# Linformer attention and squared-ReLU FFN on one core: TensorE order of the first two batches' attention rearranged, V copies of the first batch on VectorE, rest of Q loaded ahead of the last w_out piece

## The chip, the core and the metric

The kernel runs on one core of one Trainium2 chip. The metric is device time in microseconds (us).

## The reference

Eight batches, eight heads, 1024 tokens of 64 elements. Keys and values are projected from 1024 positions to 64, then comes attention, then a two-layer FFN over all tokens:

```python
k_proj = einsum('ks,bhsd->bhkd', E, k);  v_proj = einsum('ks,bhsd->bhkd', F, v)
attn = softmax(q @ k_proj.T / 8)                 # 1024 x 64 for each head
x = (attn @ v_proj) -> (8192, 512)
out = square(maximum(x @ w_in, 0)) @ w_out       # 512 -> 2048 -> 512, float32
```

## The kernel before

TensorE's instruction order is written by hand; the other engines are ordered by a scheduler. The FFN of a batch is 64 numbered steps: for each half `c` of the tokens, 16 steps of the first layer (four matmuls each) and 16 of the second layer (four each). The attention of the next batch is hung between those steps with `at(step, stage)`, which puts a stage behind the matmuls of its step. The code is condensed here. In batch 0 steps 1 to 16 are the first layer of half 0, steps 17 to 32 its second layer, 33 to 48 and 49 to 64 the same for half 1.

```python
aps = ctx.enter_context(tc.tile_pool(name="aps", bufs=2, space=PSUM))   # attention: 2 tiles of 2 banks
fps = ctx.enter_context(tc.tile_pool(name="fps", bufs=4, space=PSUM))   # FFN and the rest: 4 single banks
# ... loads, all but that of E on the GpSimd queue, in this order:
#     K0,Q0 first heads | K0,Q0 other heads | F | V0 x2 | w_in x5 | w_out x4 | rest of Q0 | K1 V1 Q1 | K2 V2 Q2 ...

def keep_k(self, ps_k, h=slice(0, 8), second=None):          # k projection out of PSUM, twice
    nc.vector.tensor_copy(self.kp[:, h, 0, :], view)
    (second or nc.vector.tensor_copy)(self.kp[:, h, 1, :], view)   # batch 0: second = nc.scalar.copy
def keep_v(self, ps_v, h=slice(0, 8)):
    nc.scalar.copy(self.vp[HI, h], view)
    nc.vector.tensor_copy(self.vp[LO, h], view)

def inverse(self, ps):                           # 1 / sum of the exponentials, on ScalarE
    nc.scalar.activation(rs[:], ps[:], AF.Ln)
    nc.scalar.activation(rs[:], rs[:], AF.Exp, scale=-1.0)

def values(self, pr, spare=False):
    e = self.e.pop(pr)
    ps_s = att_psum();  self.sums_mm(ps_s, e);  rs = self.inverse(ps_s)
    ps_x = [bank(), bank()] if spare else att_psum()
    # ... 4 matmuls into ps_x, then VectorE: xT = ps_x * rs

def store(self, c, tb, ps):                      # after each 128 rows of the output
    nc.scalar.copy(o[:], ps[:])
    nc.sync.dma_start(out_rows[self.b, i, :, :], o[:])
# ... the front, and batch 0's plan: shown in the diff below
```

Q1, V1 and so on stand for the tensors of batch 1; Q0 for those of batch 0. "The rest of Q" is the half of Q0 that belongs to the tokens of half 1.

The softmax here doesn't subtract the row's maximum and nothing guards it: scores larger than these inputs give would overflow.

## Time and profile before

The median is 522.35 us over three runs (522.2 to 522.53); the profiled span is 521.1 us.

| reading | view | value |
|---|---|---|
| TensorE busy | page, part 1 | 506.3 us of 521.1 |
| named waits of TensorE | waits | 11.1 us |
| of these, rest of Q | waits | 2.9 us, once |
| of these, attention PSUM held by the Ln | waits | 2.0 us, twice |
| after the last matmul | timeline | 3.6 us |
| rest of Q lands, last w_out piece lands | issue plus time to landing | 42.5, 40.0 us |
| Q1 lands | the same | 59.2 us |

These are the busy line of TensorE and the chain that ended last, from the page of the kernel before:

```profile
PE 506.3 (97%) x2764; PEld 223.8 (43%) x2764; DVE 174.7 (34%) x367; ACT 287.1 (55%) x428; POOL 32.2 (6%) x44
PE 90%; DMA 7%; POOL 1%; ACT 1%; DVE 0%; issue 0%; POOLq 0%
```

These are TensorE's waits in the same run (who waited, for whom, total us, times, longest us):

```profile
PE ps_bank L216 <- DMA Q_sb<-in_q_dram: 2.9, 1, 2.9
PE ps_att L241 <- ACT rs L260: 2.0, 2, 1.0
...
PE ps_bank L327 <- DVE xT L310: 1.1, 2, 0.9
...
PE ps_bank L206 <- ACT kp L171: 0.4, 1, 0.4
```

TensorE is the bound, so each of these waits is on the chain as long as nothing later waits anyway. The two upper ones look like this in the timeline (start us, duration us, engine, line, operation, in brackets the idle time before it and who ended it). First the rest of Q, at steps 19 and 20:

```profile
38.68 1.03 PE L333 MATMUL ps_bank<-w_out_126,hsq 128*128 128x512 bf16 x4
42.57 0.62 PE L216 MATMUL ps_bank<-ident,Q_sb 128*128 128x128 bf16 x8 [2.86 <-DMA Q_sb<-in_q_dram]
43.02 1.03 PE L333 MATMUL ps_bank<-w_out_126,hsq 128*128 128x512 bf16 x4
43.89 0.61 PE L216 MATMUL ps_bank<-ident,Q_sb 128*128 128x128 bf16 x8
44.33 1.89 PE L333 MATMUL ps_bank<-w_out_128,hsq 128*128 128x512 bf16 x8
```

Four matmuls of w_out end at 39.7; then TensorE is idle until Q lands, transposes it in two groups with four matmuls between, and is at step 21 at 44.33. Second, one of the two waits for the Ln (the other is like it, 0.91 us at 81.1):

```profile
74.88 0.41 PE L247 MATMUL ps_att<-expT,ones 64*64 64x512 bf16 x4
75.12 0.39 PE L281 MATMUL ps_att<-expT,vp 64*64 64x512 bf16 x4
76.55 0.41 PE L241 MATMUL ps_att<-qT,kT 64*64 64x512 bf16 x4 [1.04 <-ACT rs L260]
```

The scores (L241) need an attention PSUM tile, but the sums just written are still being read by the Ln on ScalarE, one microsecond long.

### The profile page before, as it was taken

The page shows a single profiled execution, that of the slowest core. Times are in us where ns is not written, and L with a number is a line of the kernel's source. Part 1 is how long each engine was busy: PE and PEld are TensorE (multiplying, and loading weights), DVE is VectorE, ACT ScalarE, POOL GpSimd, SP SyncE. Part 2 cuts the span into 40 slices and gives each one's busy share as a digit, 9 for nine tenths or more (in the row PEclk, how much of TensorE's full clock was granted, in tenths as well). Part 3 has the DMA queues.
Part 4 walks back from the last instruction along what each step waited for, and adds up shares of the span by engine and source line. Part 5 has one row for each costly group of instructions (what it writes and reads, how often), then busy time and mean ns, then how long its engine had stood idle before and what let it go on. Part 6 is the DMA issues. An engine that isn't in the chain of part 4 may idle for free.

```text
span 521.1 us, 6860 instructions
## 1 busy us (share of the span) xinstructions
PE 506.3 (97%) x2764; PEld 223.8 (43%) x2764; DVE 174.7 (34%) x367; ACT 287.1 (55%) x428; POOL 32.2 (6%) x44
## 2 busy tenths in 40 slices
PE   7897999999999999999999999999999999999997
PEld 3443443444444444444444444444444444444443
DVE  2351552433513244142431325232440424313130
ACT  1563475574735667276654756356662766544351
POOL 6420100120200020000100000000000000000000
PEclk9899999999999999999999999999999999999999
DMA  9999999999995099104851050110101011010102
GB/s 154 205 205 206 241 207 186 135 207 206 185 191 127 25 179 202 69 13 79 170 97 60 1 142 21 40 42 20 62 1 60 21 40 42 20 62 20 62 0 81
DMA packets 64975, 53.26 MB, mean 102 GB/s; under 512 B 26416, under 2 KB 56624, under 8 KB 64944
## 3 DMA queue, kind: packets, MB, share of 16 engines
q0 software_dynamic: 30880, 29.49, 36.1%
q1 hardware_dynamic: 34064, 23.34, 16.0%
q8 instruction: 21, 0.34, 0.3%
q14 instruction: 10, 0.08, 0.1%
HBM read 59.24 MB, written 16.78 MB: 146 GB/s over the span
## 4 chain that ended last, share of the span: by engine, by line
PE 90%; DMA 7%; POOL 1%; ACT 1%; DVE 0%; issue 0%; POOLq 0%
PE ps_bank L333 43%; PE ps_bank L327 40%; DMA Q_sb<-in_q_dram 4%; DMA w_in_116<-in_moe_w_in_dram 3%; PE ps_bank L182 2%; PE ps_att L247 2%; PE ps_att L241 2%; PE ps_att L281 1%; PE ps_bank L281 0%; PE ps_bank L206 0%; ACT rs L260 0%; POOL Q_sb L76 0%; POOL K_sb L76 0%; POOL V_sb L76 0%; PE ps_bank L216 0%
## 5 line engine op out<-in xcount | busy, mean ns | idle before, releaser
L323 ACT ACTIVATE h_relu<-ps_bank 128x512 bf16<-128x512 f32 x256 | 151.3, 599 | 63.7 <-PE ps_bank L327 62.8
L324 DVE TENSOR_TENSOR hsq<-h_relu 128x512 bf16<-128x512 bf16 x256 | 108.8, 425 | 195.0 <-ACT h_relu L323 193.7
L333 PEld LDWEIGHTS <-hsq 128*128 128x128 bf16 x1024 | 97.6, 98 | 123.2 <-issue 9.3
L340 ACT COPY o_sb<-ps_bank 128x512 f32<-128x512 f32 x64 | 37.3, 586 | 114.8 <-PE ps_bank L333 114.8
L333 PE MATMUL ps_bank<-w_out_128,hsq 128*128 128x512 bf16 x256 | 65.7, 380 | 0.0
L333 PE MATMUL ps_bank<-w_out_124,hsq 128*128 128x512 bf16 x256 | 65.6, 379 | 0.0
L333 PE MATMUL ps_bank<-w_out_126,hsq 128*128 128x512 bf16 x256 | 65.6, 379 | 0.0
L333 PE MATMUL ps_bank<-w_out_130,hsq 128*128 128x512 bf16 x256 | 65.4, 379 | 0.0
L327 PE MATMUL ps_bank<-xT,w_in_122 128*128 128x512 bf16 x256 | 59.2, 379 | 0.0
L327 PE MATMUL ps_bank<-xT,w_in_118 128*128 128x512 bf16 x256 | 58.2, 379 | 0.1
L327 PE MATMUL ps_bank<-xT,w_in_120 128*128 128x512 bf16 x256 | 58.0, 379 | 0.0
L260 ACT ACTIVATE rs<-ps_att 128x1024 f32<-128x1024 f32 x32 | 32.7, 1024 | 23.2 <-PE ps_att L247 23.1
L327 PEld LDWEIGHTS <-w_in_120 128*128 128x128 bf16 x256 | 25.0, 98 | 30.4 <-issue 0.4
L327 PEld LDWEIGHTS <-w_in_118 128*128 128x128 bf16 x256 | 24.9, 98 | 30.1 <-issue 0.4
L327 PEld LDWEIGHTS <-w_in_122 128*128 128x128 bf16 x256 | 24.4, 98 | 30.8 <-issue 2.7
L255 ACT ACTIVATE expT<-ps_att 128x1024 bf16<-128x1024 f32 x32 | 31.8, 1023 | 10.1 <-PE ps_att L241 10.1
L285 DVE TENSOR_TENSOR xT<-ps_att,rs 128x512 bf16<-128x512 f32 x32 | 20.6, 686 | 44.6 <-ACT rs L261 44.6
L261 ACT ACTIVATE rs<-rs 128x1024 f32<-128x1024 f32 x32 | 33.8, 1059 | 0.6
L285 DVE TENSOR_TENSOR xT<-ps_bank,rs 128x512 bf16<-128x512 f32 x24 | 15.5, 686 | 50.5 <-ACT rs L261 50.5
L327 PE MATMUL ps_bank<-xT,w_in_114 128*128 128x512 bf16 x128 | 30.6, 379 | 1.1 <-DVE xT L310 1.1
L327 PE MATMUL ps_bank<-xT,w_in_116 128*128 128x512 bf16 x128 | 30.4, 379 | 0.0
L327 PEld LDWEIGHTS <-w_in_114 128*128 128x128 bf16 x128 | 12.4, 98 | 16.1 <-issue 1.7
(64 smaller groups left out, 203.5 us busy)
## 6 DMA issues: line engine op xcount, KB each, us to landing
out_dram<-o_sb SPq DMA_DIRECT2D x64, 256.0 KB, 2.0
K_sb<-in_k_dram POOLq DMA_DIRECT2D x7, 1024.0 KB, 17.9
V_sb<-in_v_dram POOLq DMA_DIRECT2D x7, 1024.0 KB, 23.7
Q_sb<-in_q_dram POOLq DMA_DIRECT2D x7, 1024.0 KB, 10.8
K_sb<-in_k_dram POOLq DMA_DIRECT2D x2, 512.0 KB, 8.0
V_sb<-in_v_dram POOLq DMA_DIRECT2D x2, 512.0 KB, 12.0
Q_sb<-in_q_dram POOLq DMA_DIRECT2D x2, 256.0 KB, 8.3
w_in_118<-in_moe_w_in_dram POOLq DMA_DIRECT2D x1, 512.0 KB, 15.1
```

The source lines that it names most:

```text
L182: nc.tensor.matmul(ps[LO, :], lhsT=ET[:, i, :], rhs=self.K[:, :, i, :], start=f, stop=l)
L241: nc.tensor.matmul(ps[o, par], lhsT=self.kT[r, h, :], rhs=self.qT[r, h, n, :], start=True, stop=True)
L247: nc.tensor.matmul(ps[o, par], lhsT=ones[r, :], rhs=e[r, par], start=True, stop=True)
L255: nc.scalar.activation(e[:], ps[:], AF.Exp, scale=SCALE)
L260: nc.scalar.activation(rs[:], ps[:], AF.Ln)
L261: nc.scalar.activation(rs[:], rs[:], AF.Exp, scale=-1.0)
L285: nc.vector.tensor_tensor(out=self.xT[:, pr, :, par], in0=ps_x[par].rearrange("p (c t) -> p c t", c=2), in1=rs[:, par].rearrange("p (c t) ...
L323: nc.scalar.activation(r[:], ps[:], AF.Relu)
L324: nc.vector.tensor_tensor(out=self.hsq[c][:, fb, :], in0=r[:], in1=r[:], op=ALU.mult)
L327: nc.tensor.matmul(ps[:], lhsT=w_in_blk(cb, fb), rhs=self.xT[:, cb, c].rearrange("p a t -> p (a t)"), start=(cb == 0), stop=(cb == NCB - 1),)
L333: nc.tensor.matmul(ps[:], lhsT=self.hsq[c][:, fb, tb * P:(tb + 1) * P], rhs=w_out_blk(fb), start=(fb == 0), stop=(fb == NFB - 1),)
L340: nc.scalar.copy(o[:], ps[:])
```

## The change

The intent is to take these two waits away, and to close small gaps in the front with warm-up matmuls and a better order. The diff, with cuts marked:

```diff
     for j in range(WP):
+        if j == WP - 1:
+            load(Q0[:, :, 4:8, :], tokens(q, 0, i=slice(4, 8)))
         t = wpool.tile([P, fn, DM], BF16, name=f"w_out_{j}")
         load(t[:], w_out_view[:, j * fn:(j + 1) * fn, :])
-    load(Q0[:, :, 4:8, :], tokens(q, 0, i=slice(4, 8)))
# ...
-        def keep_v(self, ps_v, h=slice(0, 8)):
+        def keep_v(self, ps_v, h=slice(0, 8), first=None):
-            nc.scalar.copy(self.vp[HI, h], view)
+            (first or nc.scalar.copy)(self.vp[HI, h], view)
# ... in project_v, batch 0 only:
-            self.keep_v(ps[HI, 0:C // 2], half[g])
+            self.keep_v(ps[HI, 0:C // 2], half[g], nc.vector.tensor_copy)
# ... the front:
-        warm(4)
+        warm(8)
         ET = projection("ET", e_bf)
-        warm(8)
+        warm(3)
         att.project_k(0)
         att.transpose_q_chunk(0, Q0, 0)
         att.transpose_k(half[0])
+        warm(1)
         att.chunk_scores(0, 0)
+        warm(2)
         att.project_k(1)
+        att.chunk_sums(0, 0)
         att.transpose_q_chunk(0, Q0, 1)
-        att.chunk_sums(0, 0)
         att.transpose_k(half[1])
+        warm(1)
         att.chunk_scores(0, 1)
         FT = projection("FT", f_bf)
+        warm(3)
+        att.chunk_sums(0, 1)
         att.project_v(0)
-        att.chunk_sums(0, 1)
+        warm(2)
         att.chunk_values(0, 0)
+        warm(2)
         att.project_v(1)
# ... batch 0's plan:
-                at(19, att.transpose_q_chunk, 1, Q0, 0)
+                at(20, att.transpose_q_chunk, 1, Q0, 0)
                 at(20, att.transpose_q_chunk, 1, Q0, 1)
                     at(36, nxt.project)
-                    at(36, nxt.transpose_q, 0), at(36, nxt.transpose_q, 1)
+                    at(37, nxt.transpose_q, 0), at(37, nxt.transpose_q, 1)
                     at(39, nxt.transpose_k)
-                    scores 0, 1 at 42; transpose_q 2 at 44, 3 at 45
-                    values 0 and scores 2 at 47; values 1 and scores 3 at 50; values 2 at 55, 3 at 60; no spare banks
+                    scores 0, 1 at 41; transpose_q 2 and 3 at 43
+                    values 0 at 45; scores 2 at 49; values 1 (spare) and scores 3 at 51
+                    values 2 (spare) at 55, values 3 (spare) at 59
-                        at(60, coming.project), at(62, coming.transpose_q_dma)
+                        at(61, coming.project), at(63, coming.transpose_q_dma)
                         at(64, coming.transpose_k)
```

The last part is told in short form. From batch 1 on the plan is the same as before.

More of the change, by code (lines that the diff above doesn't have):

```diff
@@ L433 @@
                     at(36, nxt.project)
-                    at(36, nxt.transpose_q, 0)
-                    at(36, nxt.transpose_q, 1)
+                    at(37, nxt.transpose_q, 0)
+                    at(37, nxt.transpose_q, 1)
                     at(39, nxt.transpose_k)
-                    s1, s2, s3, s4, s5 = 42, 47, 50, 55, 60
-                    at(44, nxt.transpose_q, 2)
-                    at(45, nxt.transpose_q, 3)
-                else:
-                    s1, s2, s3, s4, s5 = 14, 18, 24, 30, 49
-                at(s1, nxt.scores, 0)
-                at(s1, nxt.scores, 1)
-                spare = b > 0
-                at(s2, nxt.values, 0, spare)
-                at(s2, nxt.scores, 2)
-                at(s3, nxt.values, 1, spare)
-                at(s3, nxt.scores, 3)
-                at(s4, nxt.values, 2)
-                at(s5, nxt.values, 3)
+                    at(41, nxt.scores, 0)
+                    at(41, nxt.scores, 1)
+                    at(43, nxt.transpose_q, 2)
+                    at(43, nxt.transpose_q, 3)
+                    at(45, nxt.values, 0)
+                    at(49, nxt.scores, 2)
+                    at(51, nxt.values, 1, True)
+                    at(51, nxt.scores, 3)
+                    at(55, nxt.values, 2, True)
+                    at(59, nxt.values, 3, True)
+                else:
+                    at(14, nxt.scores, 0)
+                    at(14, nxt.scores, 1)
+                    at(18, nxt.values, 0, True)
+                    at(18, nxt.scores, 2)
+                    at(24, nxt.values, 1, True)
+                    at(24, nxt.scores, 3)
+                    at(30, nxt.values, 2)
+                    at(49, nxt.values, 3)
                 if b + 2 < B:
                     if b == 0:
-                        at(60, coming.project)
-                        at(62, coming.transpose_q_dma)
+                        at(61, coming.project)
+                        at(63, coming.transpose_q_dma)
                         at(64, coming.transpose_k)
                     else:
-                        at(s4, coming.project)
+                        at(30, coming.project)
                         at(27, coming.transpose_q_dma)
-                        at(s5, coming.transpose_k)
+                        at(49, coming.transpose_k)
             for step, _ in enumerate(Ffn(att, b == 0).steps(), 1):
```

## The prediction

> **What bounds the kernel.** TensorE: the busy table gives PE 506.3 us of a 521.1 us span (97%), and the chain of waits is 90% PE. Its 14.8 us of idle time is 11.1 us of named waits (the waits view) plus a tail of 3.6 us (the last matmul ends at 517.5). From batch 1 on there is nothing to win (PE busy 61.0 of 61.0 us in the windows view, 97 to 158), and that schedule stays. So the change can only take waits of the first 85 us: rest of Q 2.9 us (until 42.6); att-PSUM held by the Ln of a softmax 2.0 us (1.04 at 75.5, 0.91 at 80.2); e_bf 1.9; xT 1.1; kT 0.8; FT 0.5; kp 0.4; vp 0.3.
>
> **What the change does.**
>
> 1. Rest of Q one place earlier in the load queue. Loads land in turn: w_out's last piece at 40.0 us (issued 21.05, 18.9 to landing), rest of Q at 42.5 (22.35 + 20.2). Swapped, Q should land near 40.0 and that w_out piece near 42.5. TensorE needs the piece about 43: it just fits. Both Q transposes now follow step 20, so four more matmuls (0.86 us) stand before them. Before, TensorE was through all this at 44.3. After, it comes to the transposes at 36.95 + 16 x 0.216 = 40.4 if the front gains nothing, never before 40.0; done at 40.9 to 41.3. Gain 3.0 to 3.4 us.
>
> 2. The front. Warm-up matmuls are 8+3 rather than 4+8, plus a few in gaps. 128x512 matmuls run 0.43 us apart cold and 0.216 warm here, as in the Trainium skill ("TensorE: Matmul & The Clock Gate", the clock gate: 426.7 and 215.7 ns). The first K projection starts about 1.2 us earlier (8.0, when K lands, instead of 9.17), but the second half of K (12.4), of V (19.5) and w_in (20.8, 22.1) still land as before, so little carries through. V copies were already one after the other (ScalarE 0.37, then VectorE 0.43); both on VectorE take the same, but ScalarE is free for the inverse (ended at 22.9, should end near 20). Projections of V run warm (1.1 instead of 1.4 to 1.6 us). I expect 0 to 0.6 us at step 5; anything above 0.4 is eaten by the wait for Q.
>
> 3. Second half of batch 0. Values stand further from scores and take their PSUM from the spare banks, so the two waits for Ln (1.95 us) go. Waits for banks behind copies may give back 0.2 to 0.6. Batch 1's Q landed at 59.2; its transposes come at about 59.6: little or no wait. All of it is on TensorE, so on the critical path.
>
> The sum: 3.2 + 1.95 - 0.3 = about 4.9 us.
>
> **Predicted time: 517.4 us, range 516.2 to 519.0 (8 in 10). Chances: faster by over 2% 0.01, within 2% 0.98, slower 0.01.**
>
> **What would show it.** In the waits view the wait for Q falls from 2.9 to under 0.5 us and "<- ACT rs" from 2.0 to under 0.3; w_out's last piece lands 2.5 us later than before with no wait for it; the granted clock from 13 to 26 us rises from 0.87 to above 0.95; step 21 starts near 41 instead of 44.3; from batch 1's FFN on, TensorE's timeline is shifted by about 5 us.
>
> **What would make it wrong.** The swapped piece of w_out, or batch 1's Q, arrives late and becomes the new wait; warm matmuls hold up real work; bank waits eat the Ln gain.

## The result, and the profile after

The changed kernel took 518.88 us (median of four runs, 518.74 to 520.21), the kernel before 522.36 us in the same job. The ratio is 0.9939, with a 95% interval of 0.9922 to 0.9956. A ratio here is the mean time of one kernel's fast runs over the mean of the other's fast runs of the same rounds, so it is not quite the ratio of the medians. In a second job (six runs, beside eleven of before) the changed kernel took 519.11 us and the ratio was 0.9924. The gain is 3.5 to 3.8 us by the medians; 4.9 us was predicted. 518.88 is at the slow edge of the predicted range, 519.11 just outside it; that the change is worth less than 2% was predicted too.

Line numbers of the changed kernel are one higher than before (L217 is the old L216, and so on). Its page has these lines:

```profile
PE 507.5 (98%) x2774; PEld 224.2 (43%) x2774; DVE 175.7 (34%) x369; ACT 286.1 (55%) x426; POOL 31.9 (6%) x44
PE 87%; DMA 11%; POOL 1%; issue 0%; ACT 0%; POOLq 0%
```

Its waits of TensorE:

```profile
PE ps_bank L191 <- DMA K_sb<-in_k_dram: 1.7, 1, 1.7
...
PE ps_bank L328 <- DVE xT L311: 1.1, 2, 0.9
PE ps_bank L207 <- ACT kp L172: 0.8, 1, 0.8
PE ps_bank L183 <- ACT o_sb L341: 0.6, 1, 0.6
...
PE ps_bank L227 <- DMA Q_sb<-in_q_dram: 0.6, 1, 0.6
```

Both waits that the change aimed at are gone: there is no line for L217 that waits for the rest of Q, and none for L242 that waits for the Ln. In their place one line has grown and two are new: L207 behind a copy of k on ScalarE (0.8 us; before, it was 0.4 and for the first four heads, while the second four, which wait now, did not wait), L183 behind an output copy (0.6), and L227 behind Q1 (0.6). The first line, a wait for the first K, is an accident of this run (below). Step 21 in the timeline, and the new wait for Q1:

```profile
39.91 1.89 PE L334 MATMUL ps_bank<-w_out_126,hsq 128*128 128x512 bf16 x8
41.64 1.06 PE L217 MATMUL ps_bank<-ident,Q_sb 128*128 128x128 bf16 x16
42.53 1.89 PE L334 MATMUL ps_bank<-w_out_128,hsq 128*128 128x512 bf16 x8
...
61.90 1.07 PE L227 MATMUL ps_bank<-ident,Q_sb 128*128 128x128 bf16 x16 [0.57 <-DMA Q_sb<-in_q_dram]
```

TensorE came to the rest of Q at 41.64 and did not wait; step 21 begins at 42.53, which is 1.8 us sooner than before and not the 3 us predicted. This first profile is of the slowest of the four runs (520.21 us). In it the first K landed at 8.45 us, not at 7.85 as in the profile of before, and the later loads 0.3 to 1.3 us late. So the first thing to settle was what a usual run looks like.

### The profile page after: what moved, and what is told of

The parts are those of the page before. It is cut to its first block, busy times and chain, and to the rows that moved or that the text cites. A ratio compares the mean times of both kernels' runs of the same rounds, so it can differ in the third digit from the quotient of the medians.

```text
span 518.4 us, 6881 instructions
## 1 busy us (share of the span) xinstructions
PE 507.5 (98%) x2774; PEld 224.2 (43%) x2774; DVE 175.7 (34%) x369; ACT 286.1 (55%) x426; POOL 31.9 (6%) x44
## 4 chain that ended last, share of the span: by engine, by line
PE 87%; DMA 11%; POOL 1%; issue 0%; ACT 0%; POOLq 0%
PE ps_bank L334 40%; PE ps_bank L328 39%; DMA Q_sb<-in_q_dram 8%; DMA w_in_122<-in_moe_w_in_dram 3%; PE ps_bank L183 2%; PE ps_att L248 2%; PE ps_att L242 1%; PE ps_bank L282 1%; PE ps_att L282 1%; PE ps_bank L207 0%; PE ps_bank L227 0%; POOL K_sb L76 0%; ACT o_sb L341 0%; ACT rs L261 0%; POOL Q_sb L76 0%
## 5 line engine op out<-in xcount | busy, mean ns | idle before, releaser
L286 DVE TENSOR_TENSOR xT<-ps_bank,rs 128x512 bf16<-128x512 f32 x30 | 19.3, 686 | 60.2 <-ACT rs L262 60.2
L286 DVE TENSOR_TENSOR xT<-ps_att,rs 128x512 bf16<-128x512 f32 x26 | 16.8, 687 | 33.0 <-ACT rs L262 33.0
```

The lines of the kernel that those rows point to most:

```text
L286: nc.vector.tensor_tensor(out=self.xT[:, pr, :, par], in0=ps_x[par].rearrange("p (c t) -> p c t", c=2), in1=rs[:, par].rearrange("p (c t) ...
```

## The experiments

Medians and ranges are of five or six runs unless said otherwise; the kernel before ran eleven times beside each of the first three groups, with medians of 522.94, 523.34 and 522.91 us. Times of different groups may differ by a few tenths for that reason.

My theory after the first profile had three parts. First, the front was not made faster, since the earlier sums put an Ln in front of the second k copy. Second, a PSUM bank held by an output copy costs 0.6 us at step 61. Third, the landing of Q1 now stops TensorE. The main rival was that all of this was one unlucky run.

### r_after: the changed kernel again

No edit.

> The changed kernel again, unedited. Its one profile so far was of a run of 520.2 us, its other three runs took 518.7 to 519.0. In that profile the loads landed 0.6 us late from the first one on and 1.3 us late from w_in on, and TensorE was still cold at the first K projection; step 5 began 1.24 us later than before. Theory A (the front itself was made slower, by about 0.8 us: ScalarE now runs the first Ln ahead of the second kp copy, and the V projection now waits for the softmax sums): this profile shows the kp wait of 0.8 us again, and step 5 begins at 27.2 to 27.9. Theory B (that profile was only an unlucky run): loads land as before (Q's rest at 40.0), step 5 begins at 26.0 to 26.6, and a gain of 1.2 us more than in the first profile. Time 518.8 either way.

Measured: 519.11 us (518.58 to 519.76), ratio 0.9924. The profile is of the run of 518.58 us, span 516.8. Its waits of TensorE, cut:

```profile
PE ps_bank L328 <- DVE xT L311: 1.1, 2, 0.9
PE ps_bank L207 <- ACT kp L172: 0.8, 1, 0.8
PE ps_bank L183 <- ACT o_sb L341: 0.6, 1, 0.6
```

The k wait and the bank wait are there again, and the waits for DMA are not. Loads were early (first K at 7.34, rest of Q at 39.57), and step 21 began at 41.51. Step 5 began at 26.80, in the range of neither theory. So the first profile's late loads were chance, and the two waits behind ScalarE are not. The k wait is explained by ScalarE's order. This is ScalarE before:

```profile
14.34 0.36 ACT L171 CAST kp<-ps_bank 64x256 bf16<-64x256 f32 x1 [0.40 <-DVE kp L170]
14.79 1.02 ACT L260 ACTIVATE rs<-ps_att 128x1024 f32<-128x1024 f32 x1
```

and in the first profile after:

```profile
14.67 1.02 ACT L261 ACTIVATE rs<-ps_att 128x1024 f32<-128x1024 f32 x1 [0.84 <-PE ps_att L248]
15.59 0.35 ACT L172 CAST kp<-ps_bank 64x256 bf16<-64x256 f32 x1
```

Because `chunk_sums(0, 0)` now stands ahead of the transposes, the scheduler puts its Ln (1.02 us) ahead of the second k copy, which waits it out. The Trainium skill says in "Perfetto Trace Analysis", section "Tensor Engine Instruction (MATMUL, LD_WEIGHTS)", that ScalarE's queue is strictly first in, first out; this trace agrees, for the copy starts at 15.59, as the Ln ends (14.67 + 1.02). I had the engine orders of the changed kernel in hand before I predicted and did not draw this consequence.

The bank wait at step 61 is the same kind of thing. ScalarE in r_after:

```profile
85.35 1.02 ACT L261 ACTIVATE rs<-ps_att 128x1024 f32<-128x1024 f32 x1 [1.53 <-PE ps_att L248]
86.41 1.06 ACT L262 ACTIVATE rs<-rs 128x1024 f32<-128x1024 f32 x1
87.37 0.57 ACT L341 COPY o_sb<-ps_bank 128x512 f32<-128x512 f32 x1
```

and TensorE:

```profile
87.99 0.38 PE L183 MATMUL ps_bank<-K_sb,ET 128*64 128x512 bf16 x1 [0.64 <-ACT o_sb L341]
```

The values of step 59 put an Ln and an exponential on ScalarE; the output copy of step 60 stands behind both and ends at 87.94; the projection of batch 2 needs that copy's bank and starts at 87.99. Before, those values came at step 60, behind that copy.

### x_front: the old front in the changed kernel

```diff
-        warm(8) ... the front of the changed kernel, V copies on VectorE
+        warm(4) ... the front of before, V copies on ScalarE and VectorE
```

> The changed kernel with the front of before (warm-up counts, order of sums, V copies on ScalarE), the rest changed. Theory A: the old front is faster, step 5 begins near 26.6, TensorE comes to the transposes of Q at 40.4, and the time is 0.5 to 1.0 us below r_after. Theory B: the fronts are equal within 0.3 us in typical runs, and so are the times. The prediction had the new front 0 to 0.6 us ahead.

Measured: 518.98 us (518.81 to 519.59), so 0.13 below r_after, which is nothing. The profile shows step 17 at 36.52 (37.16 in r_after), and then this:

```profile
PE ps_bank L227 <- DMA Q_sb<-in_q_dram: 0.8, 1, 0.8
```

Whatever the front wins, Q1 takes: it landed at 60.4. Later profiles with the new front have step 17 at 36.53 (y_p62), 36.93 (w_gate) and 38.51 (y_q38, where the V projection ran cold and took 1.88 us instead of 1.06). The scatter from run to run is larger than the difference between the fronts. Neither front is shown to be faster: where Q1 comes next, an equal time can't tell.

### x_queue: the rest of Q last again

```diff
-        if j == WP - 1:
-            load(Q0[:, :, 4:8, :], ...)          # ahead of the last w_out piece
+    load(Q0[:, :, 4:8, :], ...)                  # after it, as before
-                at(20, att.transpose_q_chunk, 1, Q0, 0)
+                at(19, att.transpose_q_chunk, 1, Q0, 0)
```

> The changed kernel with the rest of Q loaded last again and the transposes at steps 19 and 20; the new front and the new second half kept. Theory: the wait for Q returns in full and ends when Q lands, near 42.5 whatever the front does; the time is 2.0 to 3.0 us above r_after (3.0 was this part's share in the sum of the first profile).

Measured: 521.96 us (520.63 to 524.09), 2.85 above r_after by the medians and 2.05 by the lowest runs. As expected, the wait is back (2.5 us, until Q landed at 42.14). The large scatter has a cause that the profile shows. These are two stretches of x_queue (us, then the busy time of each engine; the third column from the end is the granted TensorE clock):

```profile
39.60:42.10 2.50, 0.07 (x1) 0.00 (x0) 0.00 (x0) 0.00 (x0) 0.00 (x0) 1.00 1.34 204
42.10:45.50 3.40, 3.32 (x20) 2.21 (x21) 0.69 (x1) 0.00 (x0) 0.00 (x0) 0.52 1.25 208
```

The first is the wait; in the 3.4 us after it TensorE was granted 0.52 of its clock. I come back to this with the repeats of before.

### x_half: the old second half of batch 0

```diff
-   scores 41, values 45 / 51 / 55 / 59 with spare banks, projection of batch 2 at 61
+   scores 42, values 47 / 50 / 55 / 60 without, projection at 60   # the plan of before
-   first transposes of Q1 at 37
+   first transposes of Q1 at 36, as before
```

> The changed kernel with the second half of batch 0 in its old order and PSUM (no spare banks). Predicted share of this part was 1.65 us; the first profile gave 1.95 won less 0.57 (batch 1's Q) less 0.64 (a bank held by an output copy) = 0.8. Theory A: the time is 0.6 to 1.0 us above r_after, and the two waits for Ln (1.0 and 0.9 us) are back. Rival: both new waits are chance (late loads) and the time is 1.5 to 2.0 us above r_after.

Measured: 520.90 us (520.59 to 523.11), 1.8 above r_after. Both waits for the Ln are back:

```profile
PE ps_att L242 <- ACT rs L261: 2.0, 2, 1.0
```

Here the rival's number came out, not mine. I had booked the Q1 wait of the first profile against this part, but the old second half meets Q1 as well (its transposes started at 59.98, as Q1 landed). This part of the prediction, 1.65 us, was nearly right. The traces give it more cleanly than the medians: from the start of step 33 to the start of the last matmul of step 64 TensorE took 39.82 us in the kernel before and in x_half, and 38.36 in r_after, where it did not wait for Q1. That is 1.46 us.

The parts do not add: 2.85 and 1.8 lost singly are 4.65, while all together win 3.83 in this group. A common cap is not what this shows: under a cap, undoing one part costs less than its size, because the other still fills the cap, and the losses would add up to less than the whole. The excess is in part the scatter of x_queue (by the lowest runs the losses are 2.05 and 2.01, the whole 3.59). In part it may be that x_half also puts Q1's transposes a step nearer to its landing. That there is a cap is seen in x_front, where a TensorE that came 0.64 us earlier to step 17 lost 0.77 us to Q1, and in the next runs.

### y_p62: batch 2's projection one step later

```diff
-                        at(61, coming.project)
+                        at(62, coming.project)
```

> The changed kernel with batch 2's projection one step later (62, not 61). Theory: the wait of 0.64 us at 61 is for the PSUM bank whose output copy stands on ScalarE behind the Ln and the exponential of the values moved to step 59; one step (four matmuls, 0.86 us) later it is free. The wait goes and the time falls by 0.5 to 0.7 us. Rival: something else (kp copies, the next transposes of K) becomes late and nothing is won (within 0.2 us).

Measured: 518.31 us (five runs 518.03 to 518.48, one of 521.0), 0.8 below r_after. The wait behind the output copy is gone from the profile. The theory holds. TensorE came to step 17 early here (36.53) and waited 1.22 us for Q1, until 60.89.

### y_q38: the first transposes of Q1 one step later

```diff
-                    at(37, nxt.transpose_q, 0), at(37, nxt.transpose_q, 1)
+                    at(38, nxt.transpose_q, 0), at(38, nxt.transpose_q, 1)
```

> The changed kernel with the first two transposes of batch 1's Q one step later (38, not 37). Theory: with the new front TensorE arrives at them as Q lands (60.26 and 60.21 in r_after), so there is no wait to take away in a typical run: within 0.3 us of the changed kernel's 519.1 (a bit lower in runs with late loads). Rival: that landing sets the time of every run, and it falls by 0.6 us or more.

Measured: 518.49 us (four runs 518.17 to 518.55, two of 520.1 and 521.4), 0.6 below r_after by the medians. That is the rival's number. The profile of r_after, with no wait for Q1, was its fastest run; in most runs, then, the landing of Q1 sets the time. This rests on the times and on the waits for Q1 in four other profiles with the transposes at 37 (0.57 us in the first one, 0.77 in x_front, 1.22 in y_p62, 1.23 in y_sums). The profiled run of y_q38 itself can't show it: it is the one of 520.1, it had the cold V projection named above, and TensorE came to Q1 late, at 62.35.

### y_sums: the first sums behind the transposes again

```diff
-        att.chunk_sums(0, 0)
         att.transpose_q_chunk(0, Q0, 1)
         att.transpose_k(half[1])
+        att.chunk_sums(0, 0)
```

> The changed kernel with the first softmax sums behind the second Q and K transposes again in program order, which puts ScalarE's second kp copy ahead of the Ln. Theory: the wait for kp of 0.8 us at 15 us falls to under 0.4, TensorE comes to the second-layer matmuls (step 17) 0.4 to 0.9 us earlier against the landing of the first loads, and then waits for batch 1's Q by about as much, so the time stays within 0.3 us of 519.1. Rival: the kp wait is not due to the Ln, and stays at 0.8.

Measured: 519.16 us (518.67 to 519.52), the same as r_after. Its waits:

```profile
PE ps_bank L227 <- DMA Q_sb<-in_q_dram: 1.2, 1, 1.2
...
PE ps_bank L207 <- ACT kp L172: 0.7, 2, 0.4
```

The k wait fell from 0.83 to two of at most 0.4 us, as expected. Step 17 began at 36.23, the earliest of all profiles, and Q1 took it back: 1.2 us. Q1 landed at 60.59 and its transposes started at 60.59. With x_front this is the second front whose head start ends at the same place.

### z_best: old front, and both repairs

```diff
+   the front of x_front, Q1's transposes at 38, batch 2's projection at 62
```

> Old front, new load order, new second half, with batch 1's first Q transposes at 38 and batch 2's projection at 62. In x_front the old front reached step 17 0.64 us before the new one in r_after and then lost 0.77 to batch 1's Q. Theory A (fronts differ, and batch 1's Q hides it): with the transposes a step later that wait is gone, as is the bank wait; the time is 1.1 to 1.4 us below x_front's 519.0, so about 517.7, and 0.5 or more below y_p62. Theory B (fronts are equal): about the same as y_p62, 518.4.

Measured: 518.55 us (517.85 to 520.66). Neither theory's number, and not decided: the loads were late in the profile (first K at 8.54, Q1 at 62.14). Its best run is 0.2 below the best of y_p62. w_both below has the same two repairs with the new front and is lower (517.72; best runs 517.61 and 517.85), so no advantage of the old front is seen.

### w_gate: the first four output stores held back

Why does Q1 land at 60.2, when it landed at 59.2 before and every load up to the last w_out piece landed later then? The gaps between landings (issue plus time to landing, from the views of the loads' tiles) say where the time goes:

| us from the landing before | before | r_after | w_gate |
|---|---|---|---|
| K1 lands at | 47.59 | 47.25 | 47.27 |
| V1 after K1 | 5.12 | 6.52 | 5.12 |
| Q1 after V1 | 6.51 | 6.44 | 5.01 |
| K2 after Q1 | 6.85 | 5.20 | 5.30 |
| first stores of the output issued | 49.1 to 57.8 | 46.2 to 55.0 | 86.4 to 88.4 |

Times to landing are given to a tenth, so these gaps are good to about 0.1 us. With no store beside it a load of this size takes 5.0 to 5.1 us (V1 and Q1 in w_gate). In r_after the two loads ahead of Q1's landing are both slow, before only one of them is. The suspicion is the four output stores of the first half: TensorE, 2.8 us earlier, sends them 2.8 us earlier. Before, the last two were issued at 56.6 and 57.5, shortly ahead of Q1's landing, and K2 behind it was slow too; in r_after they are issued at 53.8 and 54.7, and the cost of all four falls on V1 and Q1. The Trainium skill, "DMA: Bandwidth & Descriptors", section "Issuing engines are not separate DMA queues", says that transfers issued by different engines run on the same 16 DMA engines and interleave. So stores from SyncE's queue can slow loads from GpSimd's.

```diff
-    out_pool bufs=4
+    out_pool bufs=8
     def store(self, c, tb, ps):
         nc.scalar.copy(o[:], ps[:])
+        if self.cold and c == 0:
+            self.held.append((i, o)); return
+    def release(self, kp):                        # at step 38, batch 0
+        for i, o in self.held:
+            nc.vector.scalar_tensor_tensor(out=o[0:1, 0:1], in0=kp[0:1, 0, 0, 0:1], scalar=0.0,
+                                           in1=o[0:1, 0:1], op0=ALU.mult, op1=ALU.add)
+            nc.sync.dma_start(out_rows[self.b, i, :, :], o[:])
```

> The changed kernel whose first four output stores (256 KB each, issued at 46 to 56 us) are held back until batch 1's K is projected (about 61 us or later): a VectorE write of one element, which needs that K, goes into each output tile before its store (it adds 0 x K, so the result stays right); eight output buffers instead of four so that nothing else waits. Theory (batch 1's V and Q land late, 6.5 us apart instead of 5.1, because TensorE, now 2.8 us earlier, sends its stores ahead of them): V and Q of batch 1 land 5.1 to 5.3 us apart, Q lands about 2 us earlier, near 58 if the first load lands at 7.2, TensorE has no wait for it, and the time falls by 0.4 to 0.8 us against 519.1, as in y_q38 (518.5). Rival (the loads are slow there for another reason, such as batch 2's loads sharing the engines): Q lands at 60 to 61 as before.

Measured: 518.18 us, all five runs within 518.08 to 518.45, so 0.93 below r_after and with far less scatter. In r_after the stores were issued here (SyncE's queue):

```profile
46.23 8.77 SPq L343 DMA_DIRECT2D out_dram<-o_sb  x4
```

and in w_gate here; the scheduler put them behind the transposing transfer of Q2, later than I meant:

```profile
72.91 13.40 SPq L234 DMA_TRANSPOSE qT<-Q_sb  x1
86.41 1.99 SPq L354 DMA_DIRECT2D out_dram<-o_sb  x4
```

The load of Q1, the same instruction at the same time, in r_after and then in w_gate:

```profile
L76 POOL DMA_DIRECT2D Q_sb<-in_q_dram x1: 876/876/876, 29.6 to 29.6; - x1
DMA to landing us min/median/max: 30.6/30.6/30.6
```

```profile
L76 POOL DMA_DIRECT2D Q_sb<-in_q_dram x1: 873/873/873, 29.6 to 29.6; - x1
DMA to landing us min/median/max: 27.8/27.8/27.8
```

It lands 2.8 us sooner, at 57.4, and TensorE waits no more (transposes at 59.90). V1 and Q1 land 5.12 and 5.01 us apart. This is the cap: the stores that the faster TensorE sends earlier delay the load that TensorE needs next. The 0.93 us are the difference of the medians and a little more than expected. The two profiles differ by only 0.4 us (spans 516.8 and 516.4), since the profiled run of r_after had no wait for Q1; the bank wait at step 61 (0.6) is in both.

### w_both, w_bothsums, w_all: do the repairs add up

```diff
 w_both:      Q1's transposes at 38 and batch 2's projection at 62
 w_bothsums:  w_both, and the first sums behind the transposes as in y_sums
 w_all:       w_bothsums, and the held stores of w_gate
```

> The changed kernel with both repairs: batch 2's projection at 62 and batch 1's first Q transposes at 38. Each alone gave 518.3 and 518.5 against 519.1. If the two waits are independent: about 517.8 (517.5 to 518.0). Rival: they hide each other, 518.3.

> w_both, and the first sums behind the second Q and K transposes again (as in y_sums, where TensorE reached step 17 0.9 us earlier than in r_after and lost it to batch 1's Q). Theory: with that wait out of the way some of it shows: 0.3 to 0.6 us below w_both, 517.3 to 517.6. Rival: the landing of batch 1's Q (60.6 in y_sums) catches it again at 38, and it equals w_both.

> w_bothsums and the held stores of w_gate. Theory: no load holds TensorE any more after the rest of Q, so the whole 0.9 us of y_sums shows: 0.2 to 0.5 us below w_bothsums. Rival: the held stores collide with batch 2's loads or keep ScalarE waiting for output buffers, and it is slower than w_bothsums.

Measured: w_both 517.72 us (five runs 517.61 to 517.93, one of 519.25), ratio 0.9898. That is 1.39 below r_after, and the two repairs alone gave 0.80 and 0.62; they are independent. w_bothsums 517.82 (517.35 to 518.97), no better than w_both, so that expectation failed; its profiled run had late loads (first K at 8.94), and I cannot say from it whether they or Q1 ate the gain. w_all 517.35 (516.93 to 519.94), ratio 0.9888 with an interval of 0.9867 to 0.9909. It is 0.47 below w_bothsums by the medians, as expected, but the runs overlap. It is the lowest median, but w_both is nearly as good and simpler. The profile of each of these three is of its slowest run, so what its usual run looks like was not seen. All four kernels of this group beat both the kernel before and the changed one by their medians.

### b_again1 to b_again4: the kernel before, four more profiles

The eleven runs of before in each group fall into two sets, 522.2 to 523.3 and 523.95 to 524.7. Why was still open after the other runs, so the kernel before was profiled four more times.

> The kernel before, unedited, for one more profile. Theory: in a run of the upper group (524.2 or more) the granted clock is about 0.5 for some 3 us after the wait for the rest of Q, or for some 3 us in the front, and a run of the lower group (522.2 to 523.3) has neither. Rival: the upper group has late loads (first K after 8.3 us) and full clock.

> As b_again1: a second profile of the kernel before, to be put into one of the two groups by its time and read for the clock after the wait for Q.

> As b_again1: a third profile of the kernel before, to be put into one of the two groups by its time and read for the clock after the wait for Q.

> As b_again1: a fourth profile of the kernel before, to be put into one of the two groups by its time and read for the clock after the wait for Q.

Measured, one run each: 522.54, 522.34, 522.53 and 524.51 us. Two stretches of b_again1, the wait for the rest of Q and the 3.4 us after it:

```profile
39.50:42.10 2.60, 0.68 (x4) 0.10 (x1) 0.00 (x0) 0.00 (x0) 0.00 (x0) 1.00 1.35 203
42.10:45.50 3.40, 3.26 (x27) 1.99 (x28) 1.38 (x2) 0.00 (x0) 0.87 (x1) 1.00 1.24 208
```

The same of b_again4:

```profile
39.50:42.10 2.60, 0.03 (x1) 0.00 (x0) 0.00 (x0) 0.00 (x0) 0.00 (x0) 1.00 1.36 203
42.10:45.50 3.40, 2.99 (x20) 1.89 (x21) 0.69 (x1) 0.00 (x0) 0.00 (x0) 0.63 1.24 208
```

In b_again4, TensorE's clock was granted at 0.63 after the wait, in the other three it was 1.00. In b_again4 step 33 began at 58.31, in b_again1 at 56.37: 1.94 us, which is the whole difference in time (1.97). Of this, 0.27 is a later landing of the rest of Q (transposes at 42.51 and 42.24); the other 1.67 is the clock. The first K was equally early in both (7.14 and 7.34), so the rival falls. The irony is that b_again4 had the faster front, with a full clock from 13 to 20 us where b_again1 had 0.85. It came to the rest of Q 0.65 us sooner, waited 2.98 us instead of 2.06, and lost its clock. Only one profile of the upper set was caught, so the link is shown once, and a second time in x_queue.

The Trainium skill, "TensorE: Matmul & The Clock Gate", sections "What's actually happening" and "HAM oscillation", says that the clock is halved after a window of about 3.4 us of idleness, and that the window runs freely, so its phase differs from run to run. The traces agree on the window: the granted clock is 0.50 for one stretch of 3.41 us (42.23 to 45.65 in x_queue, 42.97 to 46.38 in b_again4) and 1.00 on both sides of it. They agree on the phase, and show that the length of the wait alone does not decide: 2.51 us of waiting cost the clock in x_queue, while 2.86 us in the first profile of before did not. In the 3.41 us just ahead of the slow stretch TensorE was busy for 0.90 us in x_queue and 0.46 in b_again4. In the first profile of before, whose clock had last changed at 20.75 us, the stretches of 3.41 us counted from there meet at 41.23, in the middle of the wait, and TensorE was busy for 1.89 us of the one and 2.07 of the other.

## Why the prediction was right or wrong

1. **The rest of Q: right in mechanism, a little too large.** Predicted 3.0 to 3.4 us at step 21; r_after shows 44.33 - 41.51 = 2.82. The wait is gone, the w_out piece that gave up its place landed at 42.20 and was first used at 43.89, as expected. The upper end needed a faster front, which did not come. x_queue, which undoes this part alone, gives 2.85 by the medians and 2.05 by the lowest runs.

2. **The front: no gain seen.** Of "0 to 0.6 us at step 5" nothing is seen: step 5 began at 26.59 before and at 26.80 in r_after, and x_front shows no difference in time. The V projections do run warm in r_after (1.06 us) and the granted clock from 13 to 26 us is 1.00, as predicted, but not in every run: it is 0.87, as before, in the profiles of x_half, y_q38 and w_both, which have the new front. The earlier sums put an Ln ahead of a k copy (0.83 us of waiting at a place where there was none), and whether the first K projection is cold remains a matter of chance (1.92 us in r_after, 1.03 in y_p62).

3. **The second half: right for the waits, too low on what comes back.** The two waits for the Ln (1.95 us) are gone in every profile of the changed kernel. The bank term was counted as 0.3 and measured 0.64 in one wait, at step 61. Predicted for the part was 1.65 us; the traces give 1.46, x_half by the medians 1.8.

4. **The step that failed: "Batch 1's Q landed at 59.2; its transposes come at about 59.6: little or no wait."** It took a landing from the old trace and held it fixed, while the change moved the stores that share the DMA engines with it. In r_after Q1 landed at 60.21 although the loads up to K1 were about 0.3 us earlier than before. TensorE waited for it for 0.57 to 1.23 us in four profiles. Holding the stores back brought it to 57.40 and the time down by 0.93 us; moving the transposes behind it won 0.6.

The sum was 3.2 + 1.95 - 0.3 = 4.9 us. In the profile of r_after, its fastest run, it is 2.82 + 1.46 = 4.28 us, and the two spans differ by 4.3 (521.1 and 516.8): so 0.6 us of the miss are two terms that were a little too large. In the usual run Q1 takes another 0.6 (y_q38) to 0.9 us (w_gate), which leaves 3.4 to 3.7, beside gains of 3.5 and 3.8. And w_both, which takes away the bank wait and the wait for Q1, is at 517.7, close to the 517.4 predicted; but that is another kernel and does not make the prediction right.

What is not in the prediction at all is the scatter of before. The change takes away the wait that sometimes costs the clock; by the means, which the ratio uses, some part of the gain is that. In the group of r_after the five slower of the eleven runs raise the mean of before by 0.76 us; if all five lost their clock as b_again4 did, which one profile shows, that is the share. In the first job before had no such run.

## What to carry to other kernels

When a change makes the bounding engine faster, ask what it will then send earlier, and which load that transfer will meet: a landing time read from the old trace does not stay where it was. Undo each part alone, but read the traces and not only the sum of the losses: a common cap makes that sum smaller than the whole, and scatter can make it larger. A cap shows itself where a head start is lost again at the same wait. On an engine that works in order, as ScalarE here, look at what a reordered producer puts in front of a short copy that TensorE waits for.

## What the Trainium skill lacked or had wrong

- "TensorE: Matmul & The Clock Gate", section "Why this matters for your kernels", gives about 3 us of idleness between bursts of matmuls as the limit. Here a wait of 2.51 us (x_queue) was followed by a granted clock of 0.52 for 3.4 us, and one of 2.86 us by 1.00. The page doesn't say how busy a window may be and still count as idle: 0.90 of 3.41 us busy lost the clock, 1.89 did not. It cost 1.7 us in b_again4.
- "DMA: Bandwidth & Descriptors", section "Issuing engines are not separate DMA queues", says that transfers issued by different engines interleave on the same DMA engines. The section has no figure for what stores cost loads: here four stores of 256 KB put 2.8 us on two loads of 1 MB (6.52 + 6.44 against 5.12 + 5.01 us).
- I found no page with the run-to-run spread of the first load. In these profiles the first K, issued at about 1.25 us each time, landed between 6.94 and 8.94 us. Later loads moved with it only in part: with the new order of loads the rest of Q landed at 41.0 to 41.4 us in the three profiles with the first K after 8.4, and at 39.3 to 39.9 in the others, the one with the first K at 8.0 among them.
